# First batch's blocks enter the first layer five tiles later through a buffer of their own; unused work credit is kept and spent at up to three units a tile

## The chip, the cores and the metric

The kernel runs on one core of a Trainium2 chip. The metric is the device time of one execution in microseconds; lower is better. The engines named here are TensorE (PE, with its weight loads PEld), VectorE (DVE), ScalarE (ACT), GpSimd (POOL) and SyncE (SP), whose queue issues every DMA of this kernel.

## What is computed

Attention with queries averaged in pairs, then two feed-forward layers one after the other, all in float32 at the boundary:

```python
# q, k, v: (4, 8, 1152, 64); q_pool: (4, 8, 576, 64)
q_pool = q.reshape(B, H, S // 2, 2, D).mean(axis=3)
scores = np.matmul(q_pool, k.transpose(0, 1, 3, 2)) / np.sqrt(D)
attn = np.exp(scores - scores.max(-1, keepdims=True))
attn = attn / (attn.sum(-1, keepdims=True) + 1e-9)
x = np.matmul(attn, v)                    # -> (2304 tokens, 512)
h = x @ w_in;  g = h * np.cos(h);              x = g @ w_out    # layer 1, 512 -> 2048 -> 512
h = x @ w_in2; g = h * (1 / (1 + np.exp(-h))); x = g @ w_out2   # layer 2, 512 -> 2048 -> 512
```

## The kernel before

Every float32 operand of a matrix product is split into a high and a low float16 part, and three of the four partial products are taken.

**Attention.** A pair is one batch with heads j and j + 4; there are 16 pairs, four to a batch, numbered 0 to 15 here. A pair has nine tiles of 128 query rows, so the 144 tiles run in four batches of 36. For one tile: TensorE makes the scores (`sp`, L546; the fifth tile of a pair holds the rest of both heads and has twice the instructions, L554), VectorE scales them and takes the maximum (`sc`, L565), ScalarE takes the exponential (L573) and then the high part (`hl`, L579), GpSimd the low part (`hl`, L151), SP transposes both by DMA (`hlT<-hl`, L586), and TensorE multiplies by the values (`pv`, L597 and L601). `hl` is a ring of four buffers. The preparation of the next pair (`qn`, `kn`, `vt`, L467 and L472, and the transposes `qT`, `kT`) runs between the tiles as a background generator.

**Layer 1.** A finished batch gives two blocks of 256 tokens (blocks 0 and 1 from batch 0, up to 6 and 7 from batch 3), and the leftover rows of all batches give a ninth. A block has 16 H units (L682, twelve matmuls of 256 columns each) and 16 Y units (L742, also twelve). After two H units ScalarE takes two copies out of PSUM (`hk` L699, `tt` L703); after four of them come VectorE's steps (L716, L725, L730), a sine on ScalarE (L722) with a switch of its function table before it and one back to the exponential after it, and GpSimd's low part `gl`. The Y units of a block follow its H units by 12 units (`LG`). Before its first unit a block is split by `x_split`: maximum, scale, `xn` (ScalarE L664 and VectorE L665) and a DMA transpose `xT<-xn` (L668). In the kernel before, `xn` is taken from the `hl` ring.

**Who sets the order.** The tile loop (at L1070 and after) writes the program: scores, exponential, high and low part, then `advance()`, which steps every background generator once, and `share()`, which emits layer-1 units from a credit. `advance()` is called four times a tile. In batches 1 to 3 each half tile adds one credit (`RATE` is 2 a tile). A unit spends one; credit is capped at 4, and when no block is in `blocks_q` the units wait. A block of batches 1 to 3 waits another 40 steps (`X_LAG`, ten tiles) after `x_split` before it is put in `blocks_q`; blocks 0 and 1 do not wait. A scheduler then reorders each engine's queue by priorities, so the built order differs from the written one, but each engine runs its own queue in order.

**After attention** come the remaining units of layer 1, in a loop that takes one unit and one step of the preparation of layer 2's weights (`wgen2`), and then layer 2 (`ys`, `gs`, `op`).

Of the kernel before, what the change touches and what calls it, by code (L numbers as in the profile page):

```python
# [12 lines left out]
F16 = mybir.dt.float16  # L13
# [12 lines left out]
PSH = 15.0  # L26
NB_SC, NB_H, NB_T, NB_S = 4, 4, 4, 5
LOW_HL, LOW_G, LOW_W = 3, 2, 2
X_LAG = 40
W1_BUFS, WT_BUFS = 3, 3  # L30
W1_TABLE = (6, (0, 2, 4, 8, 11), 2)
W2_BUFS, W2_PACE = 3, 6
# [16 lines left out]
def attention_moe_moe_kernel(ctx, tc, q, k, v, w_in1, w_out1, w_in2, w_out2, out):  # L49
# [6 lines left out]
    DM, DFF = w_in1.shape  # L56
# [569 lines left out]
    def moe_pools(stack):  # L626
        mp = Weights()
        mp.p = stack.enter_context(tc.tile_pool(name="moe", bufs=2, reuse_waits="tile"))
        return mp
# [24 lines left out]
    def x_split(at, mp, x32, i, blk, w):  # L654

        m = small.tile([128, 1], F32, name="xm", tag="xm")
        absmax(m, x32, AX.XY)
        yield
        s = small.tile([128, 1], F32, name="xs", tag="xs")
        u = small.tile([128, 1], F32, name="xu", tag="xu")  # L660
        yield from early(scale_steps(m, ps_h, (s, u), 14), P_CH)
        blk.c = x_scale_consts(w, s, u, True)
        xn = at.p.tile([128, 2, 2, DM], F16, tag="hl", name="xn", bufs=NB_H)
        nc.scalar.activation(out=xn[:, 0], in_=x32, func=AF.Copy, scale=s)  # L664
        nc.vector.scalar_tensor_tensor(out=xn[:, 1], in0=x32, scalar=s, in1=xn[:, 0], op0=ALU.mult, op1=ALU.subtract)  # L665
        yield
        blk.T = mp.p.tile([128, 2, 2, NC, 128], F16, tag="x%d" % i, name="xT", bufs=1)
        nc.sync.dma_start_transpose(  # L668
            out=blk.T.rearrange("p e t c k -> p (e t c) k"), in_=xn.rearrange("p e t d -> p (e t d)")
        )  # L670
        blk.xh = lambda c: blk.T[:, 0, :, c, :]
        blk.xl = lambda c: blk.T[:, 1, :, c, :]
# [210 lines left out]
    if True:  # L883
# [6 lines left out]
        at = att_pools(att_stack)  # L890
# [3 lines left out]
        make_consts()  # L894

        state = Weights()
        state.mp = None
        state.ng, state.tail = 0, False
        state.psw = ps_h
        W2 = new_w("2", 8, True)  # L900
        state.credit = 0.0
        bg = []
        blocks_q = []

# [5 lines left out]
        def finish(g):  # L910
            while g in bg:
                advance()
# [35 lines left out]
        units = layer1()  # L948

        def share(x):  # L950
            if state.mp is None:
                return
            state.credit = min(state.credit + x, 4.0)
            while state.credit >= 1 and next(units, False):
                state.credit -= 1

        pairs = [(b, j) for b in range(B) for j in range(NP)]
# [27 lines left out]
        xgens = {}  # L985

        def block_steps(b, i):
            blk = Block()
            blk.g = []
            blk.ydst = ydr[2 * b + i]  # L990
            yield from early(x_split(at, state.mp, x32.pop((b, i)), i, blk, W1), P_X)
            if b:
                for _ in range(X_LAG):
                    yield
            blocks_q.append(blk)

        def x_of(b, i):
# [6 lines left out]
        def block_done(b, i):  # L1004
            if state.mp is None:
                finish(wg)
                wst_stack.close()
                state.mp = moe_pools(moe_stack)
            xgens[b, i] = block_steps(b, i)
            bg.append(xgens[b, i])  # L1010

# [40 lines left out]
        for n, (b, j) in enumerate(pairs):  # L1052


            seq = list(range(2 * NT))
            if j == NP - 1:
                seq = [t + NT * e for t in range(NT) for e in range(2)]
            seq.insert(NT, 2 * NT)
            order = []
            for o in range(0, len(seq), GT):  # L1060
                G = Pair()
                G.P, G.tiles = P.get(n), seq[o:o + GT]
                order += [(G, i, t) for i, t in enumerate(G.tiles)]
            if n + 1 < len(pairs):
                bg.append(prep_then_load(n + 1))
            else:
                at.src_stack.close()
                w2st_stack = ExitStack()
                w2st = w2st_stack.enter_context(tc.tile_pool(name="w2st", bufs=1, reuse_waits="tile"))
                wgen2 = layer2_weight_steps(W2, (w_in2, w_out2), w2st, lambda: state.psw, nc.sync, W2_BUFS, W2_TABLE)  # L1070
                bg.append(slowly(islice(wgen2, 4), W2_PACE))
            for idx, (G, gi, t) in enumerate(order):
                with ahead(P_SC):
                    T = tile_scores(at, P[n], t)
                T.G, T.gi = G, gi
                inflight.append(T)
                with ahead(P_EX):
                    tile_exp(at, T)
                tile_hi(at, T, b == 0 or (idx % HI_N) < HI_A)
                tile_lo(at, T)  # L1080
                advance()
                share(RATE[b] / 2)
                advance()
                if len(inflight) > LAG:
                    drain_pv()
                advance()
                share(RATE[b] / 2)
                advance()
# [184 lines left out]
```

## Time and profile before

| | us |
|---|---|
| median of the 3 runs shown | 1331.56 (1325.54 to 1332.42) |
| the profiled execution, whole | 1323.71 |
| its span, first to last instruction | 1321.9 |
| attention, batch 0 (tiles 0 to 35) | 0 to 231.4 |
| batch 1 (tiles 36 to 71) | 231.4 to 427.0 |
| batch 2 (tiles 72 to 107) | 427.0 to 603.1 |
| batch 3 (tiles 108 to 143) | 603.1 to 784.6 |
| rest of layer 1, then layer 2 | 784.6 to 1321.9 |

A stage begins here with the first exponential (L573) of its first tile and ends with that of the next stage; the last boundary is the exponential of the last tile. The busy time of TensorE counts each matmul from its start to its modelled end, and matmuls overlap; what one costs in a full queue is the distance from its start to the next one's.

### The profile page before, as it was taken

To read this page: it belongs to the slowest core of one execution; us is meant where nothing else is said; L and a number is where in the kernel's file an instruction comes from. 1 tells how busy PE (TensorE), PEld (TensorE's weight loads), DVE (VectorE), ACT (ScalarE), POOL (GpSimd) and SP (SyncE) were. 2 spreads that over 40 slices of the span, in tenths; PEclk is the share of its full clock that TensorE was granted. 3 is DMA by queue.
4 is the path that set the end of the run, shared out by engine and by line. 5 is a ranking of instruction groups with operands and counts; after the bars stand their busy time and mean duration, and the time that the engine had idled before them with its cause. 6 is when DMAs were issued, how large, how long until landed. Compare 5 with 4: busy or idle time off the path is not lost. (4 is left out here: it accounts for less than half of the span.)

```text
span 1321.9 us, 26728 instructions
## 1 busy us (share of the span) xinstructions
PE 1130.4 (86%) x10668; PEld 912.1 (69%) x10668; DVE 953.3 (72%) x1876; ACT 938.5 (71%) x1147; POOL 708.6 (54%) x624
## 2 busy tenths in 40 slices
PE   2565566889897789899989999899988999999998
PEld 1343343577685567676767679788877888888887
DVE  7787888777776877896779866976677754544483
ACT  4887988789887889997999884664556534443351
POOL 1768677668877667786868882444777100000000
PEclk9766665899999889998999899999999999999999
DMA  9899999868899999998999974413534000000001
GB/s 294 174 221 219 235 250 192 141 146 163 149 214 193 193 185 190 201 172 181 203 199 188 202 136 104 129 55 65 108 94 97 17 33 33 9 9 17 17 34 32
DMA packets 491165, 181.57 MB, mean 137 GB/s; under 512 B 447520, under 2 KB 465952, under 8 KB 491040
## 3 DMA queue, kind: packets, MB, share of 16 engines
q1 hardware_dynamic: 491040, 179.87, 65.5%
q8 instruction: 83, 1.36, 0.4%
q14 instruction: 42, 0.34, 0.1%
HBM read 66.58 MB, written 9.44 MB: 58 GB/s over the span
## 5 line engine op out<-in xcount | busy, mean ns | idle before, releaser
L151 POOL TENSOR_TENSOR hl<-sc,hl 128x384 f16<-128x384 f32 x432 | 450.7, 1074 | 125.6 <-ACT hl L579 92.6
L546 PE MATMUL sp<-kT,qT 128*128 128x512 f16 (+1 forms) x768 | 197.8, 378 | 85.5 <-DVE sc L565 73.9
L565 DVE TENSOR_SCALAR_CACHE_REDUCE sc<-sp,psu 128x512 f32<-128x512 f32 (+1 forms) x288 | 228.2, 808 | 58.3 <-PE sp L546 45.9
L682 PEld LDWEIGHTS <-ih 128*128 128x128 f16 x2304 | 225.5, 99 | 48.4 <-issue 18.1
L597 PE MATMUL pv<-vt,hlT 128*128 128x130 f16 (+1 forms) x1440 | 192.3, 237 | 49.8 <-DMA hlT<-hl 43.2
L573 ACT ACTIVATE sc<-sc,nb 128x1152 f32<-128x1152 f32 x144 | 179.2, 1250 | 46.4 <-DVE nb L570 33.1
L682 PE MATMUL h<-ys,ih 128*128 128x256 f16 x1152 | 194.0, 273 | 8.5 <-ACT gs L699 8.5
L597 PEld LDWEIGHTS <-hlT 128*128 128x128 f16 (+1 forms) x1440 | 146.7, 110 | 78.5 <-DMA hlT<-hl 50.6
L682 PE MATMUL h<-xT,ih 128*128 128x256 f16 x1024 | 188.0, 278 | 7.0 <-ACT tt L703 5.1
L601 PE MATMUL pv<-vt,hlT 128*128 128x65 f16 (+1 forms) x1440 | 182.7, 207 | 0.0
L546 PEld LDWEIGHTS <-qT 128*128 128x128 f16 x768 | 77.5, 110 | 152.0 <-issue 100.0
L579 ACT ACTIVATE hl<-sc 128x1152 f16<-128x1152 f32 x144 | 164.4, 1154 | 8.8 <-DMA hlT<-hl 4.6
L742 PE MATMUL y<-gh,oh 128*128 128x256 f16 x576 | 158.6, 275 | 4.8 <-ACT y L751 4.8
L742 PE MATMUL y<-gl,oh 128*128 128x256 f16 x576 | 158.5, 275 | 2.1 <-POOL gl L151 2.1
L856 PEld LDWEIGHTS <-op 128*128 128x128 f16 x1512 | 147.9, 98 | 17.9 <-issue 0.6
L742 PE MATMUL y<-gh,ol 128*128 128x256 f16 x576 | 158.6, 275 | 0.0
L682 PE MATMUL h<-ys,il 128*128 128x256 f16 x576 | 157.0, 273 | 0.0
L601 PEld LDWEIGHTS <-hlT 128*128 128x128 f16 (+1 forms) x1440 | 142.5, 108 | 16.1 <-issue 8.1
L682 PE MATMUL h<-xT,il 128*128 128x256 f16 x512 | 142.5, 278 | 0.0
L151 POOL TENSOR_TENSOR gl<-tt,gh 128x512 f16<-128x512 f32 (+1 forms) x60 | 102.8, 1728 | 60.8 <-DVE gh L730 58.6
L742 PEld LDWEIGHTS <-oh 128*128 128x128 f16 x1152 | 112.6, 99 | 24.2 <-issue 7.0
L682 PEld LDWEIGHTS <-il 128*128 128x128 f16 x1152 | 113.6, 99 | 15.2 <-issue 0.3
(311 smaller groups left out, 2007.7 us busy)
## 6 DMA issues: line engine op xcount, KB each, us to landing
wst<-in_moe_w_in_dram SPq DMA_DIRECT2D x16, 1024.0 KB, 6.4
stk<-in_k_dram SPq DMA_DIRECT2D x32, 288.0 KB, 4.2
stv<-in_v_dram SPq DMA_DIRECT2D x32, 288.0 KB, 4.3
stq<-in_q_dram SPq DMA_DIRECT2D x32, 256.0 KB, 3.2
wst<-in_moe_w_out_dram SPq DMA_DIRECT2D x8, 1024.0 KB, 6.2
wst<-in_moe_w_out_dram SPq DMA_DIRECT2D x16, 512.0 KB, 6.3
ydr<-y SPq DMA_DIRECT2D x9, 512.0 KB, 3.6
y32b<-ydr SPq DMA_DIRECT2D x9, 512.0 KB, 3.3
```

The source lines that it names most:

```text
L151: last = nc.gpsimd.tensor_tensor(out=lo[:, o:o + w], in0=x[:, o:o + w], in1=hi[:, o:o + w], op=ALU.subtract)
L546: nc.tensor.matmul(sp[:, o - a:o - a + n], P.qT[e][:, t, :], kT[:, o:o + n], start=(e == 0), stop=(e == 1))
L565: nc.vector.tensor_scalar(out=T.sc[:, a:z], in0=sp, scalar1=T.P.su, scalar2=None, op0=ALU.mult, op1=ALU.min, accum_out=mx[:, x:x + 1],)
L573: nc.scalar.activation(out=T.sc, in_=T.sc, func=AF.Exp, scale=-1.0, bias=nb)
L579: nc.scalar.activation(out=hi, in_=T.sc, func=AF.Copy)
L597: nc.tensor.matmul(G.pv[r, T.gi], T.hlT[:, 0, c, r], P.vt[i][:, c], start=(c == 0), stop=(c == KC - 1), skip_group_check=True,)
L601: nc.tensor.matmul(G.pv[r, T.gi, 0], T.hlT[:, 1, c, r], P.vt[i][:, c, 0], start=False, stop=(c == KC - 1), skip_group_check=True,)
L682: nc.tensor.matmul(hp, wt[:, c, f * 128:(f + 1) * 128], xt(c), start=(i == 0), stop=(i == 3 * NC - 1), skip_group_check=True,)
L742: nc.tensor.matmul(blk.y[:, oc, :], wt[:, f, oc * 128:(oc + 1) * 128], gt[:, f % 4, :], start=(f == 0 and e == 0 and oc % 2 == 0), stop=(f ...
L856: nc.tensor.matmul(bank, t[:, e, c, :], wt[:, c, :], start=start, stop=True, skip_group_check=True)
```

## The change

The wait before a block enters layer 1 becomes `(20, 40)`: 20 steps, five tiles, for batch 0's blocks, 40 as before for the others. `xn` comes from a pool of its own with one buffer from the first finished block until the last pair of heads begins, so the blocks of batches 0 to 2 no longer take a buffer of the `hl` ring; those of batch 3 still do. The credit is capped at 14 instead of 4, and a half tile spends at most 1 or 2 of it in turn, so a tile at most 3.

```diff
-X_LAG = 40
+X_LAG = (20, 40)
...
-        xn = at.p.tile([128, 2, 2, DM], F16, tag="hl", name="xn", bufs=NB_H)
+        if state.xp is None:
+            xn = at.p.tile([128, 2, 2, DM], F16, tag="hl", name="xn", bufs=NB_H)
+        else:
+            xn = state.xp.tile([128, 2, 2, DM], F16, name="xn", bufs=1)
...
-            state.credit = min(state.credit + x, 4.0)
-            while state.credit >= 1 and next(units, False):
+            state.credit = min(state.credit + x, 14.0)
+            state.turn = 3 - state.turn
+            for _ in range(state.turn):
+                if state.credit < 1 or not next(units, False):
+                    return
                 state.credit -= 1
...
-            if b:
-                for _ in range(X_LAG):
-                    yield
+            for _ in range(X_LAG[b > 0]):
+                yield
...
+                state.xp = xn_stack.enter_context(tc.tile_pool(name="xn", bufs=1, reuse_waits="tile"))
...
             else:
                 at.src_stack.close()
+                for i in range(2):
+                    finish(xgens[b - 1, i])
+                xn_stack.close()
+                state.xp = None
```

Three places in the built order. The first is ScalarE's queue at the start of batch 1, from the exponential of tile 39 on. `xn` is the split of a block, `qn`, `kn`, `vt` and `qT` are the preparation of pair 5, `hk` and `tt` are the copies that follow H units. Before:

```order
L573 ACTIVATE sc<-sc,nb 128x1152
L664 ACTIVATE xn<-x_532,xs 128x1024
L579 ACTIVATE hl<-sc 128x1152
L620 ACTIVATE x_533<-pvs,den 128x64 x3
L573 ACTIVATE sc<-sc,nb 128x1152
L579 ACTIVATE hl<-sc 128x1152
L573 ACTIVATE sc<-sc,nb 128x1152
L579 ACTIVATE hl<-sc 128x1152
L573 ACTIVATE sc<-sc,nb 128x1152
L699 ACTIVATE hk<-h,ca 128x512
L703 ACTIVATE tt<-h,quarter,ca 128x512
```

After:

```order
L573 ACTIVATE sc<-sc,nb 128x1152
L467 ACTIVATE qn<-stq,ps__2447 128x9x64
L467 ACTIVATE kn<-stk,ps__2447 128x9x64 x2
L467 ACTIVATE vt<-stv,ps__2447 128x9x64
L579 ACTIVATE hl<-sc 128x1152
L467 ACTIVATE vt<-stv,ps__2447 128x9x64
L620 ACTIVATE x_533<-pvs,den 128x64 x3
L573 ACTIVATE sc<-sc,nb 128x1152
L579 ACTIVATE hl<-sc 128x1152
L667 ACTIVATE xn<-x_532,xs 128x1024
```

The preparation of pair 5, which stood behind the first two sines before, now stands ahead of the first block's `xn`, and the first `hk` has moved back by nine rows of this queue.

The second place is ScalarE's queue around the second block's `xn`, a few tiles later in batch 1. Before, it is followed by three rows `hl` that share its ring:

```order
L573 ACTIVATE sc<-sc,nb 128x1152
L722 ACT_TABLE_LOAD
L722 ACTIVATE tt<-tt,halfpi 128x1024
L664 ACTIVATE xn<-x_533,xs 128x1024
L579 ACTIVATE hl<-sc 128x1152 x3
L699 ACTIVATE hk<-h,ca 128x512
L703 ACTIVATE tt<-h,quarter,ca 128x512
```

After:

```order
L573 ACTIVATE sc<-sc,nb 128x1152 x2
L620 ACTIVATE x_2669<-pvs,den 128x64 x2
L667 ACTIVATE xn<-x_533,xs 128x1024
L579 ACTIVATE hl<-sc 128x1152 x2
L573 ACTIVATE sc<-sc,nb 128x1152
L702 ACTIVATE hk<-h,ca 128x512
L706 ACTIVATE tt<-h,quarter,ca 128x512
```

Both blocks are now split before the first H unit is copied out, and the sine stands behind them.

The third place is TensorE's queue just after the last attention tile, where `bm` is a small product that spreads a column's maximum over the partitions (`xm` of block 7, `mrem` of the leftover rows, `mw` of a weight piece). Before, Y units stand between these and the first H unit:

```order
L742 MATMUL y<-gh,ol_86 128x256
L110 MATMUL bm<-xm,mean 128x1
L110 MATMUL bm<-mrem,mean 128x1
L742 LDWEIGHTS oh_85
L742 MATMUL y<-gh,oh_85 128x256
L742 LDWEIGHTS oh_85
L742 MATMUL y<-gl,oh_85 128x256
```

After:

```order
L745 MATMUL y<-gh,ol_86 128x256
L110 MATMUL bm<-ym,mean 128x1
L110 MATMUL bm<-mw,mean 128x1
L110 MATMUL bm<-xm,mean 128x1
L110 MATMUL bm<-mrem,mean 128x1
L110 MATMUL bm<-mw,mean 128x1
L685 LDWEIGHTS ih_83
L685 MATMUL h<-xT,ih_83 128x256
```

The five small products now stand together, with 13 matmuls of Y units between them and the last `pv` (84 before the first H unit in the kernel before), and block 6's 16 H units follow them in one run.

## Rows read from the trace of the kernel before

**Rows 1.** The page's head: the span, and the engines' busy time

```profile
span 1321.9 us, 26728 instructions
PE 1130.4 (86%) x10668; PEld 912.1 (69%) x10668; DVE 953.3 (72%) x1876; ACT 938.5 (71%) x1147; POOL 708.6 (54%) x624
```

**Rows 2.** Busy time by stretch (batches 1, 2, 3, rest); last columns: clock, DMA, GB/s

```profile
231.40:427.00 195.60, 169.12 (x1697) 129.37 (x1694) 145.74 (x326) 166.75 (x199) 146.56 (x132) 0.97 0.86 167
427.00:603.10 176.10, 152.72 (x1595) 116.86 (x1596) 141.11 (x315) 163.69 (x199) 128.51 (x124) 0.93 1.01 192
603.10:784.60 181.50, 168.56 (x1688) 128.39 (x1686) 148.62 (x316) 161.58 (x193) 140.43 (x125) 0.95 0.93 182
784.60:1321.90 537.30, 515.45 (x4752) 458.57 (x4749) 329.49 (x486) 263.48 (x361) 140.38 (x95) 1.00 0.22 55
```

**Rows 3.** The same view for pairs 4, 7 and 11 (columns PE, PEld, DVE, ACT, POOL)

```profile
231.40:294.40 63.00, 52.80 (x506) 40.52 (x504) 45.42 (x103) 50.40 (x61) 38.64 (x35) 0.92 0.74 141
392.30:427.00 34.70, 25.97 (x279) 19.01 (x277) 25.18 (x66) 27.48 (x34) 26.98 (x27) 0.96 0.95 185
562.00:603.10 41.10, 38.50 (x424) 30.45 (x424) 34.47 (x75) 40.63 (x51) 33.84 (x32) 1.00 1.03 190
```

**Rows 4.** Timeline of ScalarE in pair 4: start, duration, in brackets idle time before

```profile
251.69 1.25 ACT L573 ACTIVATE sc<-sc,nb 128x1152 f32<-128x1152 f32 x1 [0.54 <-DVE nb L570]
257.57 0.69 ACT L699 ACTIVATE hk<-h,ca 128x512 f32<-128x512 f32 x1 [4.62 <-PE h L682]
...
260.19 0.69 ACT L699 ACTIVATE hk<-h,ca 128x512 f32<-128x512 f32 x1 [1.26 <-PE h L682]
...
280.59 3.26 ACT L579 ACTIVATE hl<-sc 128x1152 f16<-128x1152 f32 x3
...
290.29 1.16 ACT L579 ACTIVATE hl<-sc 128x1152 f16<-128x1152 f32 x1 [3.73 <-DMA xT<-xn]
```

**Rows 5.** Timeline of GpSimd in pair 4

```profile
266.90 2.89 POOL L151 TENSOR_TENSOR gl<-tt,gh 128x512 f16<-128x512 f32 x2 [12.97 <-DVE gh L730]
278.28 1.40 POOL L477 TENSOR_TENSOR stq<-stq 128x576 f32<-128x576 f32 x1 [8.49 <-DMA stq<-in_q_dram]
281.88 11.35 POOL L151 TENSOR_TENSOR hl<-sc,hl 128x384 f16<-128x384 f32 x9 [2.20 <-ACT hl L579]
```

**Rows 6.** Timeline of TensorE: a tile's scores, then values; a Y unit's start and its successor's

```profile
259.99 1.14 PE L546 MATMUL sp<-kT,qT 128*128 128x512 f16 x6
260.96 0.22 PE L597 MATMUL pv<-vt,hlT 128*128 128x130 f16 x1
...
261.94 0.38 PE L682 MATMUL h<-xT,ih 128*128 128x256 f16 x2
...
784.39 0.27 PE L742 MATMUL y<-gh,oh 128*128 128x256 f16 x1
...
785.70 0.38 PE L682 MATMUL h<-xT,ih 128*128 128x256 f16 x2
```

**Rows 7.** ScalarE's groups in batches 1 to 3: count, busy us and mean ns

```profile
L703 ACT ACTIVATE tt<-h,quarter,ca 128x512 int32<-128x512 f32 x47 | 35.8, 768 | 1.7 <-DMA ydr<-y 1.5 <-POOL gl L151 0.2
L699 ACT ACTIVATE hk<-h,ca 128x512 f32<-128x512 f32 x47 | 31.7, 675 | 11.4 <-PE h L682 11.3
L722 ACT ACT_TABLE_LOAD x22 | 28.2, 1283 | 0.4
L573 ACT ACT_TABLE_LOAD x22 | 28.2, 1283 | 6.5 <-DVE den L613 3.0 <-DVE pm L489 1.8 <-DVE nb L570 1.3
...
L722 ACT ACTIVATE tt<-tt,halfpi 128x1024 f32<-128x1024 f32 x23 | 26.4, 1148 | 1.7 <-DVE tt L716 1.5
```

**Rows 8.** After the last tile: last `pv`, block 7's maximum, TensorE's first longer wait

```profile
799.84 0.19 PE L601 MATMUL pv<-vt,hlT 128*128 128x65 f16 x1
...
804.61 1.22 DVE L128 TENSOR_REDUCE xm<-x 128x1 f32<-128x1024 f32 x1 [0.31 <-ACT x L620]
...
831.45 0.38 PE L682 MATMUL h<-xT,ih 128*128 128x256 f16 x2 [2.14 <-ACT tt L703]
```

More of the change, by code (lines that the diff above doesn't have):

```diff
@@ L896, in attention_moe_moe_kernel @@
         state = Weights()
-        state.mp = None
+        state.mp = state.xp = None
+        xn_stack = ExitStack()
         state.ng, state.tail = 0, False
@@ L901, in attention_moe_moe_kernel @@
         state.credit = 0.0
+        state.turn = 1
         bg = []
```

## The prediction, made before the changed kernel ran

> **What bounds the kernel now.** I read the page's head first [rows 1], then busy time by stretch, since no engine is the bound over the whole span. After the last tile TensorE is busy 515 of 537 us (last of [rows 2]): there time follows its matmuls. In batches 1 to 3 nothing is full over a batch: ScalarE has 166.8 of 195.6, 163.7 of 176.1 and 161.6 of 181.5 us [rows 2]. Pair by pair it looks different. Pair 11, with 15 units, has ScalarE busy 40.63 of 41.10 us; pair 7, with no H unit, has it busy 27.48 of 34.70 [rows 3]. So a pair with many H units is bound by ScalarE, and one with none has a floor of about 34.7 us that no single engine fills. Then I looked at batch 1, which is longest though its units are no more than in batch 2. Its first pair takes 63.0 us with ScalarE busy only 50.4 [rows 3]. The timelines show why: after the exponential at 251.69 ScalarE waits 4.62 us for TensorE to finish a run of H units and 1.26 us for the next, and later 3.73 us because `hl` wants a buffer that the block's `xn` still holds, until its transpose has landed [rows 4]. GpSimd has no attention tile from about 254 to 282: it waits 12.97, 8.49 and 2.20 us [rows 5]. Call this the hole.
>
> **Prices.** A unit costs TensorE 1.31 us (784.39 to 785.70), a tile 0.97 for the scores and 0.98 for the values [rows 6]; nine tiles with the odd tile's second set make 19.5 us a pair. An H unit costs ScalarE (0.768 + 0.675) / 2 = 0.72 for the copies, 1.148 / 4 = 0.29 for the sine, and 44 table loads of 1.283 over 92 units (23 sines) = 0.61, together 1.62 us [rows 7]. With pair 7's 27.5 as the base, 8 H units give 27.5 + 13.0 = 40.5, against 40.63 in pair 11 [rows 3], so the price fits. A pair's floor is then the largest of 19.5 + 1.31 x units, 27.5 + 1.62 x H units, and 34.7.
>
> **Part 1: the start of batch 1 (lag of five tiles, own buffer).** In the new order the preparation of pair 5 comes ahead of the blocks' split, both blocks are split before the first `hk`, and no `hl` row has to wait for `xn`. The wait of 3.73 us goes. The two waits behind a run of H units (4.62 and 1.26) should go too: before, the units were overdue in the written order when the transposed block arrived, and TensorE's queue has four and then eight of them in a row; now runs of four remain, but the next tiles stand ready ahead of them. That is 9.6 us of ScalarE's idle time, the engine that sets the pace here. Bounds: nothing, if the hole only moves to pair 5; and 24.8 us, which is all that batch 1 takes above the floors of its four pairs (46.9 + 45.3 + 42.1 + 36.5 = 170.8, from units counted in TensorE's order, against 195.6). The whole hole as GpSimd sees it is 23.7 us [rows 5], close to that end; but ScalarE did the units' and the preparation's work in it, which has to be done anyway, so I take the 9.6. The new buffer is single: the second `xn` waits for the first one's transpose. Between them ScalarE has about nine rows, some 9 us by its durations in [rows 4] and [rows 7], so I cost this wait at nothing; if that cover were gone it would be up to the 3.7 us that was saved, once in a batch, with exponentials queued behind it. SP's queue keeps its transposes; `xT` moves behind `qT` and `kT`, which are wanted first. The lag itself delays nothing that anyone waits for: batch 1's units still end at about tile 62 of the written order, seventeen tiles before the next block is due.
>
> **Part 2: kept credit, up to three units a tile.** This takes no work away; it packs it. In TensorE's new order the pairs of batch 1 have 4, 29, 18 and 13 units (15, 19, 17, 13 before), those of batch 2 have 4, 17, 20, 14 (3, 13, 17, 13), those of batch 3 have 14, 16, 20, 15 (18, 14, 16, 15). With the prices above the floors go from 170.8 to 172.2, 164.4 to 166.5 and 168.7 to 169.2: +4.0 us. The dense pairs are then bound by TensorE as much as by ScalarE (45.8 and 43.8 us for pair 10), where ScalarE alone was; the pairs with few units sit on the 34.7 us floor and give nothing back. What batches 2 and 3 take above their floors now (11.7 and 12.8 us) I leave as it is. Bounds: 0 (the floors' model adds too much), and +8 us for each of batches 2 and 3, half of the 16.1 us that pair 4 takes above its floor of 46.9, if their new dense pairs run as unevenly as pair 4 did. The nearest row is pair 11, which runs evenly with two units a tile, so I take +4.0.
>
> ScalarE's order has two more table loads (49 against 47): 2 x 1.283 = 2.6 us [rows 7], which is in the 0.61 per unit. The Trainium skill (ScalarE: Activation LUTs, What ACT_TABLE_LOAD costs) adds a drain of about 1.38 us to each switch, 2.66 us in all; by that the two would cost 5.3 us. The traced groups show 0.4 us of idle time before 22 loads [rows 7], so the drain isn't seen there and I go by the row.
>
> **Part 3: what is left after attention.** After the last tile's first score matmul TensorE has 404 H and 768 Y matmuls of layer 1's paired blocks in the old order, 384 and 668 in the new: 120 fewer at 1.31 / 12 = 0.109 us, 13.1 us, where TensorE sets the time. Not all of it is kept, as these units covered something. Block 7's chain from the last `pv` (799.84) to the end of its maximum (804.61 + 1.22) takes 5.8 us [rows 8]; 84 Y matmuls (9.2 us) covered it, now 13 (1.4 us). TensorE stands at the five `bm` for 1.7 us (a chain of bare durations, about 3.1) to 4.4 us: I take 3.0. All H units queue behind. Then block 6's 16 H units run in one piece, 21.0 us, while ScalarE's rows for them, with layer 2's weight pieces in between, sum to some 26 us; with two PSUM tiles of slack I take 3.6 us of waiting, less the 2.1 us that stood at this place before [rows 8], +1.5. Together -13.1 + 3.0 + 1.5 = -8.6. Bounds: -13.1 and 0.
>
> **Sum.** -9.6 + 4.0 - 8.6 = -14.2 us. The profiled execution took 1323.7 us, span 1321.9 [rows 1]; it would come to 1309.5. The median shown, 1331.56, lies 7.9 us above that execution. I take the difference from the median: 1317.4 us. With its own bounds the forecast spans 1308 to 1325.
>
> **Rivals.** (a) *The hole moves to pair 5.* For it: pair 5's order has 19 H units, more than pair 4 ever had, and runs of four still stand ahead of scores. Against: its tiles have their preparation done. Then part 1 gives 0: 4.0 - 8.6 = -4.6, 1327.0 us. Much the same comes if part 3 gives nothing because layer 2's weights are ready last: -9.6 + 4.0 = -5.6, 1326.0. Both are within 0.5% of the median (1324.9 to 1338.2), about what a measurement of this kernel can tell from no change. (b) *Slower: packing costs more than it moves.* One mechanism: at three units a tile TensorE runs units while VectorE waits for scores, and each dense start of batches 1 to 3 pays a hole. Batch 1 then keeps its own; batches 2 and 3 pay 8.05 each (half of 16.1): 16.1 + 4.0 - 8.6 = +11.5, 1343 us. It decides from 5.6 us each, which takes the sum past +6.6 us. For it: pair 4 shows that price [rows 3]. Against: the first ten tiles of batches 2 and 3 have nearly the same H units in both orders.
> The Trainium skill (Perfetto Trace Analysis, Optimization Strategy) says that stages with different bounds may gain from being interleaved; packing parts them, into tiles with three units and tiles with none. By that rule the time would come out as in (b); the trace agrees in direction, as pairs 7 and 11 show, but the +4.0 of part 2 is all that its rows give.
> (c) *More is gained*: batch 1 loses all its excess and part 3 is kept whole: -24.8 + 4.0 - 13.1 = -33.9, 1298 us. For it: GpSimd's hole is that long [rows 5]. (d) *The kept credit finds no work*: in the written order the blocks are used up at tile 140 with 8 credits left, so at most a few units more could leave the end. This is in part 3's count already and no case of its own.
>
> **How the numbers follow.** Forecast 0.50, (c) 0.10, (a) 0.26, (b) 0.14. Faster by over 0.5%: 0.60; within: 0.26; slower: 0.14. The range runs from 1302, inside (c), to 1338, which takes in (a) and leaves out most of (b).
>
> **What would show it.** Right: in pair 4 no wait of `hl` for `xT<-xn`, no idle time over 3 us of ScalarE or over 6 us of GpSimd between tiles 39 and 46, batch 1 at 183 to 191 us; batches 2 and 3 within 4 us of 176 and 181; the rest after the last exponential 7 to 11 us shorter, with a wait of 2 to 4 us at the five `bm`. Wrong: pair 5 above 66 us (the hole moved), pairs 10 or 14 above 50 (packing), or the rest unchanged in length with longer waits of `h` for ScalarE.

## The result, and the profile of the changed kernel

The changed kernel takes 1340.93 us (median of 4 runs, 1335.01 to 1343.96), the kernel before 1328.55 in runs beside it: a ratio of 1.0106, 95% interval 1.007 to 1.0143. It is about 1% slower, outside the range of 1302 to 1338, and close to the 1343 us of rival (b). The profiled execution took 1335.01 us.

The page's head, against [rows 1]: TensorE's and ScalarE's work is nearly the same, the span is 11.3 us longer.

```profile
span 1333.2 us, 26712 instructions
PE 1130.7 (85%) x10668; PEld 909.0 (68%) x10668; DVE 960.8 (72%) x1876; ACT 943.3 (71%) x1149; POOL 693.0 (52%) x624
```

Busy time by stretch (batches 1, 2, 3, rest; after the length come PE, PEld, DVE, ACT, POOL, then clock, DMA share, GB/s), against [rows 2]:

```profile
232.60:428.50 195.90, 171.38 (x1715) 130.54 (x1714) 147.39 (x327) 168.04 (x200) 135.47 (x132) 0.93 0.86 169
428.50:614.50 186.00, 168.00 (x1668) 125.19 (x1666) 144.00 (x316) 168.52 (x203) 137.10 (x128) 0.95 0.95 180
614.50:803.10 188.60, 170.72 (x1747) 131.94 (x1747) 150.05 (x320) 164.02 (x197) 133.54 (x126) 0.96 0.94 182
803.10:1333.20 530.10, 501.27 (x4596) 446.15 (x4593) 323.71 (x479) 258.86 (x353) 131.74 (x90) 0.99 0.21 53
```

These windows begin 0.6 us after the exponentials that mark the stages (231.95 for batch 1, 802.5 for the last tile). That leaves the batches' lengths as they are, but the rest is 530.7 us from its mark. So batch 1 is what it was (195.6 to 195.9 us), batch 2 is 9.9 us longer, batch 3 is 7.1 longer, and the rest is 6.6 shorter. A stage of one profile is good to a few us only: batch 0, where the kernels with whole transposes run the same work, took between 201.3 and 207.6 us in their profiles. Two kernels below whose engines run the same rows in the same order in all their stages (lag and lag20) differ by 0.7 to 2.1 us in batches 1 to 3 and by 4.3 in batch 0.

The same view for pairs 4, 5, 10 and 14 of the changed kernel:

```profile
232.60:274.50 41.90, 30.65 (x260) 20.42 (x259) 35.19 (x87) 36.01 (x44) 31.21 (x32) 0.76 0.93 164
274.50:339.10 64.60, 60.08 (x618) 49.25 (x616) 48.31 (x92) 56.18 (x66) 40.52 (x39) 1.00 0.81 163
517.50:571.30 53.80, 51.27 (x489) 38.46 (x486) 37.95 (x82) 46.06 (x54) 39.89 (x38) 0.97 0.86 159
708.30:763.70 55.40, 51.66 (x502) 38.80 (x499) 42.92 (x84) 49.20 (x58) 43.09 (x40) 1.00 0.91 183
```

and for pairs 5, 10 and 14 of the kernel before:

```profile
294.40:339.80 45.40, 38.33 (x382) 29.75 (x382) 35.05 (x76) 42.51 (x51) 39.09 (x36) 1.00 0.91 179
520.10:562.00 41.90, 38.11 (x403) 30.03 (x400) 36.65 (x77) 40.59 (x50) 32.33 (x33) 0.96 1.03 201
700.80:742.20 41.40, 39.85 (x434) 31.94 (x433) 35.86 (x72) 40.75 (x47) 35.62 (x34) 1.00 1.08 215
```

Pair 4 fell from 63.0 us [rows 3] to 41.9, but pair 5 rose from 45.4 to 64.6, with TensorE busy 60.08 of it. Pairs 10 and 14 rose from 41.9 and 41.4 us to 53.8 and 55.4; TensorE is busy 95% and 93% of them, ScalarE no longer all the time. The granted clock isn't the cause: it is 0.97 and 1.00 there, 0.96 and 1.00 before. The other pairs of batches 2 and 3 changed by -4.1 to +2.0 us, by 9 us downward together. So in this profile the loss of batches 2 and 3 sits in two pairs, each the third of its batch.

What the engines wait for in pair 10 of the changed kernel (the waits: total us, times, longest):

```profile
POOL hl L151 <- ACT hl L579: 6.7, 1, 6.7
DVE sc L565 <- PE sp L546: 6.4, 1, 6.4
POOL gl L151 <- DVE gh L733: 5.0, 2, 3.8
ACT hk L702 <- PE h L685: 3.4, 1, 3.4
```

and in pair 10 of the kernel before, the waits of the same two readers of scores and of `hl`:

```profile
DVE sc L565 <- PE sp L546: 2.2, 2, 1.6
POOL hl L151 <- ACT hl L579: 1.6, 2, 1.2
```

VectorE stands 6.4 us once for a tile's scores, until 528.30, while TensorE works off units and value products, and ScalarE then stands 3.4 us for H units (until 530.06). GpSimd's wait of 6.7 us comes 22 us later (until 551.07), behind ScalarE's part of the next pair's preparation, and doesn't follow from this one. In pair 14 the wait for scores is 4.1 us at one place, where the longest before was 0.8. That is the mechanism of rival (b), but in the third pair of a batch, not at its dense start. The first four tiles of pair 10, one line each:

```profile
517.50:524.80 7.30, 7.30 (x55) 4.67 (x52) 3.76 (x8) 7.24 (x8) 7.30 (x7) 1.00 0.87 163
524.80:532.00 7.20, 7.20 (x63) 5.27 (x63) 2.33 (x6) 3.72 (x5) 4.81 (x6) 1.00 0.45 84
532.00:538.20 6.20, 6.20 (x65) 4.36 (x64) 5.49 (x13) 6.11 (x6) 4.84 (x4) 1.00 0.52 95
538.20:545.00 6.80, 6.80 (x76) 5.60 (x74) 6.03 (x12) 6.80 (x12) 4.72 (x5) 1.00 0.74 117
```

TensorE is busy all 27.5 us of them, with 11 of the pair's 20.9 units in these tiles; in the five tiles after them it is busy 23.8 of 26.3 us. Before, the whole pair had 15.4 units.

### The profile page after: what moved, and what is told of

Read it like the earlier page. It is cut to its first block, busy times and chain, and to the rows that moved or that the text cites. A ratio compares the mean times of both kernels' runs of the same rounds, so it can differ in the third digit from the quotient of the medians.

```text
span 1333.2 us, 26712 instructions
## 1 busy us (share of the span) xinstructions
PE 1130.7 (85%) x10668; PEld 909.0 (68%) x10668; DVE 960.8 (72%) x1876; ACT 943.3 (71%) x1149; POOL 693.0 (52%) x624
## 5 line engine op out<-in xcount | busy, mean ns | idle before, releaser
L151 POOL TENSOR_TENSOR hl<-sc,hl 128x384 f16<-128x384 f32 x432 | 443.7, 1058 | 132.4 <-ACT hl L579 97.0
L685 PE MATMUL h<-xT,ih 128*128 128x256 f16 x1024 | 192.4, 281 | 8.3 <-ACT tt L706 5.9
L597 PEld LDWEIGHTS <-hlT 128*128 128x128 f16 (+1 forms) x1440 | 144.2, 109 | 69.9 <-DMA hlT<-hl 42.8
L601 PE MATMUL pv<-vt,hlT 128*128 128x65 f16 (+1 forms) x1440 | 185.5, 205 | 0.0
L601 PEld LDWEIGHTS <-hlT 128*128 128x128 f16 (+1 forms) x1440 | 140.3, 107 | 15.7 <-issue 6.6
L151 POOL TENSOR_TENSOR gl<-tt,gh 128x512 f16<-128x512 f32 (+1 forms) x60 | 92.5, 1558 | 72.8 <-DVE gh L733 72.8
```

The source lines that it names most:

```text
L151: last = nc.gpsimd.tensor_tensor(out=lo[:, o:o + w], in0=x[:, o:o + w], in1=hi[:, o:o + w], op=ALU.subtract)
L597: nc.tensor.matmul(G.pv[r, T.gi], T.hlT[:, 0, c, r], P.vt[i][:, c], start=(c == 0), stop=(c == KC - 1), skip_group_check=True,)
L601: nc.tensor.matmul(G.pv[r, T.gi, 0], T.hlT[:, 1, c, r], P.vt[i][:, c, 0], start=False, stop=(c == KC - 1), skip_group_check=True,)
L685: nc.tensor.matmul(hp, wt[:, c, f * 128:(f + 1) * 128], xt(c), start=(i == 0), stop=(i == 3 * NC - 1), skip_group_check=True,)
```

## The experiments

Eighteen kernels ran; the six that leave work out stand further down. "Y units carried" is the number of Y matmuls between the first exponential of batch 1 and the last one, divided by 12; the length is that of batches 1 to 3, both from one profile of each. Of the paired blocks' 128 H and 128 Y units every kernel carries 95 or 96 H units there.

| kernel | what it is | ratio to before (95%) | Y carried | batches 1, 2, 3 (us) | sum |
|---|---|---|---|---|---|
| before | | 1 | 82.2 | 195.6, 176.1, 181.5 | 553.2 |
| after | whole change | 1.0106 (1.007 to 1.0143) | 89.1 | 195.9, 186.0, 188.6 | 570.5 |
| lag | lag alone | 0.9926 (0.9902 to 0.9949) | 82.3 | 194.2, 178.2, 174.7 | 547 |
| lag20 | lag of 5 tiles everywhere | 0.9939 (0.9917 to 0.9962) | 82.2 | 192.1, 178.9, 176.5 | 548 |
| buf | buffer alone | 0.9958 (0.9936 to 0.998) | 83.2 | 197.1, 176.3, 178.8 | 552 |
| lag_buf | lag and buffer | 0.997 (0.995 to 0.9991) | 83.0 | 192.6, 176.8, 177.0 | 546 |
| credit | credit part alone | 1.0086 (1.0057 to 1.0116) | 90.0 | 198.5, 187.4, 188.6 | 575 |
| keep | cap of 14 alone | 1.01 (1.0069 to 1.0131) | 90.2 | 198.6, 190.4, 187.9 | 577 |
| turn | limit of 3 a tile alone | 1.0051 (1.0028 to 1.0074) | 82.0 | 196.1, 180.4, 177.3 | 554 |
| pack2 | credit part in batch 2 alone | 1.0096 (1.0074 to 1.0118) | 83.1 | 196.4, 186.0, 177.3 | 560 |
| rate225 | 2.25 credits in batch 3 | 1.0038 (1.0021 to 1.0054) | 86.5 | 199.1, 175.1, 187.8 | 562 |
| even | one unit a half tile | 1.0138 (1.0117 to 1.0158) | 80.0 | 199.6, 186.2, 181.8 | 568 |
| spread | lag, 1.75 credits in batches 1, 2 | 0.9978 (0.9959 to 0.9996) | 82.2 | 187.5, 177.8, 184.3 | 550 |
| spread1 | lag, 1.75 credits in batch 1 | 0.9964 (0.9943 to 0.9985) | 83.2 | 189.6, 173.7, 183.1 | 546 |

### The parts of the change

**lag**: in the kernel before, nothing else than

```diff
-X_LAG = 40
+X_LAG = (20, 40)
...
-            if b:
-                for _ in range(X_LAG):
-                    yield
+            for _ in range(X_LAG[b > 0]):
+                yield
```

> The lag alone: xn from the hl ring, old credit. Theory H with the buffer as its cause: batch 1 within 4 us of before, as hl still waits for xn. Theory H with the lag as its cause: batch 1 shorter by 6 to 12 us. Theory P: within 5 us of before as a whole.

**buf**: the buffer of its own, no lag (`X_LAG = (0, 40)`), old credit.

> The own buffer alone: no lag for the first batch, old credit. Theory H with the buffer as its cause: the wait of hl for xT<-xn (3.7 us) is gone and batch 1 is shorter by 3 to 10 us. Theory P: within 5 us of before as a whole. Theory L: slower, as the second xn waits for the first one's transpose on ScalarE.

**lag_buf**: the changed kernel with the old credit,

```diff
-            state.credit = min(state.credit + x, 14.0)
-            state.turn = 3 - state.turn
-            for _ in range(state.turn):
-                if state.credit < 1 or not next(units, False):
-                    return
+            state.credit = min(state.credit + x, 4.0)
+            while state.credit >= 1 and next(units, False):
```

> The lag of five tiles and the own buffer for xn, with the old credit (cap 4, no packing). Theory P (packing pays nothing back: the credit alone makes the slowdown): batches 2 and 3 return to about 176 and 181 us, batch 1 stays near 196 or a little below; the whole is 0 to 10 us faster than before. Theory H (the prediction's part 1, a gain of about 10 us hidden by the credit's cost): batch 1 is 183 to 191 us and the whole 8 to 14 us faster. Theory L (the lag or the buffer costs something too): slower than before by over 3 us.

**credit**: these lines the other way, in the kernel before.

> The kept credit with up to three units a tile alone: first batch's blocks enter at once, xn from the hl ring. Theory P: slower than before by 10 to 16 us, with batches 2 and 3 longer by about 10 and 7 us, the rest after attention about 7 us shorter, batch 1 as before (195.6 us). Theory H: slower by over 18 us. Theory L: slower by under 6 us.

Lag and buffer gain 0.3 to 0.7%; the credit alone gives most of the loss, 1.0086 of 1.0106. The lag alone is faster than both kernels, 1317.7 us: more than the 5 us that its theory P allowed, and not by theory H, since batch 1 is 1.4 us shorter instead of 6 to 12. In its profile the gain sits in batch 3 (181.5 to 174.7 us); no run here shows why. buf took 0.4% off the whole and nothing off batch 1, where 3 to 10 us were expected. Its batches 2 and 3 and those of credit:

```profile
425.60:603.80 178.20, 155.51 (x1648) 120.10 (x1645) 143.71 (x321) 163.83 (x200) 132.25 (x125) 0.97 1.03 192
603.80:778.50 174.70, 160.01 (x1673) 123.79 (x1673) 143.86 (x313) 160.33 (x191) 138.99 (x123) 1.00 0.98 185
```

```profile
432.20:619.60 187.40, 168.22 (x1683) 125.85 (x1682) 142.95 (x316) 169.52 (x204) 131.78 (x126) 0.95 0.92 179
619.60:808.20 188.60, 169.12 (x1710) 130.43 (x1711) 146.62 (x319) 163.57 (x194) 132.72 (x126) 0.96 0.92 178
```

The lag carries some 25.6 Y units in batch 2 (308 matmuls, 19 units before), one more than credit (24.6), without its loss: 6.5 of them fall into pair 8, where no block of the batch is ready yet. So it isn't the number in a batch.

**lag20**: `X_LAG = (20, 20)`, the blocks of all batches five tiles late.

> The lag alone (no buffer, old credit), with five tiles for the blocks of every batch instead of five and ten: the units of batches 2 and 3 start five tiles earlier, at two a tile, so more units leave the end without packing. Theory P: the whole is faster than with the lag alone (1317.7) by 0 to 10 us. Theory M: no gain over the lag alone, or a loss, as moved units cost as much in attention as they save at the end.

In the traces its order is that of lag row for row on TensorE, ScalarE, VectorE and GpSimd. It ran like lag, and says nothing on the later batches' lag; what it gives is a second profile of the same order.

### Which half of the credit part

**pack2**: credit, but in batch 2 only (against credit; the lines that keep the batch's number in `state.b` are left out):

```diff
-            state.credit = min(state.credit + x, 14.0)
+            pack = state.b == 2
+            state.credit = min(state.credit + x, 14.0 if pack else 4.0)
...
-            for _ in range(state.turn):
+            n = state.turn if pack else 4
+            for _ in range(n):
```

> The kernel before with the kept credit and up to three units a tile in batch 2 alone; batches 1 and 3 spend as before. Theory P (packing itself costs): batch 2 is longer by 8 to 12 us, batch 3 about as before or a few us shorter, the whole slower by 4 to 12 us. Theory M (what costs is the units moved from the end into attention): nearly nothing is moved from the end, so the whole is within 3 us of before.

**keep**: the kernel before with

```diff
-            state.credit = min(state.credit + x, 4.0)
+            state.credit = min(state.credit + x, 14.0)
```

> Half of part 2 alone: credit is kept up to 14 units, with no limit on what a half tile spends. In TensorE's order batch 2 has 25.6 Y units in place of 16, pairs 9 and 10 have 19 and 15 units, and 14 units fewer are left after attention (32 H and 57 Y against 35 and 64). Theory T (units brought into pairs that TensorE or ScalarE fills cost their full price): as slow as credit, 1338 to 1343 us, with batch 2 at 184 to 188. Rival (the limit of three a tile, which cuts units into alternating pieces, makes the loss): 1320 to 1330.

**turn**: the cap stays at 4;

```diff
-            while state.credit >= 1 and next(units, False):
+            state.turn = 3 - state.turn
+            for _ in range(state.turn):
+                if state.credit < 1 or not next(units, False):
+                    return
                 state.credit -= 1
```

> The other half alone: credit capped at 4 as before, and one or two units spent in a half tile in turn. Batch 1 and the rest after attention are those of the kernel before; in batches 2 and 3 hardly a unit more is emitted before the end, and pair 10 has 20 units in TensorE's order (17 before). Theory T: near the kernel before, 1326 to 1333, with pair 10 some 3 us longer. Rival (the limit makes the loss): 1338 or more.

**rate225**: `RATE = (0, 2, 2, 2.25)`.

> The kernel before with 2.25 credits a tile in batch 3 instead of 2, cap 4: the end keeps as many units as in the changed kernel in the written order, with the added units spread evenly over batch 3. Theory M: batch 3 is longer by 7 us or more, the rest shorter by 4 to 7, the whole slower than before or the same. Theory P: batch 3 longer by under 4 us, the whole the same or up to 4 us faster.

Keeping the credit makes the loss: keep is as slow as the whole change, with batch 2 at 190.4 us (184 to 188 expected). The limit alone costs half a per cent. pack2 points to a loss without more units in all: it carries 83.1 Y units, but 5.6 of batch 3's in batch 2, which takes 9.9 us longer, while batch 3 gives 4.2 back. The other 9 us by which its profile is longer than that of the kernel before lie outside batches 2 and 3: 4.3 in batch 0, whose order is the same, 0.8 in batch 1, and 4.0 after attention, where some two units fewer were left. rate225 carries 4.3 units more, in the full batch 3, for 6.3 us there, and gives 1.4 back after attention, where 4 to 7 were expected. The Y units of batch 2 in the kernel before, the changed kernel and keep (the window of that line alone; PE and its count):

```profile
427.00:603.10 176.10, 31.42 (x228) 21.81 (x228) 0.93 1.01 192
```

```profile
428.50:614.50 186.00, 41.15 (x299) 28.83 (x299) 0.95 0.95 180
```

```profile
429.70:620.10 190.40, 44.21 (x320) 31.66 (x320) 0.95 0.94 182
```

**even**: credit left from a wait isn't spent in one burst:

```diff
-            while state.credit >= 1 and next(units, False):
+            if state.credit >= 1 and next(units, False):
```

> The kernel before with at most one unit a half tile (no burst of four when blocks arrive): less packing, and three H units more at the end. Theory P: batches 2 and 3 the same or shorter by up to 6 us, the rest longer by 2 to 4 us, the whole within 4 us of before. Theory M: attention shorter by as much as the rest is longer or more, the whole up to 4 us faster. Too close to tell the two apart alone; it shows whether the packing price goes on below two units a tile.

**spread** and **spread1**: lag with `RATE = (0, 1.75, 1.75, 2)` and `(0, 1.75, 2, 2)`.

> The opposite of packing: the lag alone (blocks 0 and 1 five tiles later, old credit), and 1.75 credits a tile in batches 1 and 2 in place of 2, so that units of a batch run on into the first pair of the next one, where no block is ready yet. In TensorE's order pair 10 has 11 units (20 with the lag alone), pair 8 has 15 (11), pair 12 has 17 (15), and the rest after attention is unchanged (35 H and 64 Y). Theory T (units cost their price in pairs that are full and little in those that are not): batch 2 at 172 to 177, the whole at 1308 to 1316, faster than the lag alone (1317.7). Rival (density makes no difference by itself, the lag gained only by closing the hole): within 0.2% of the lag alone, 1315 to 1321.

> The lag alone with 1.75 credits a tile in batch 1 only. Pair 8 has 15 units in TensorE's order (11 with the lag alone), pair 10 has 18 (20), the rest after attention is unchanged. Theory T: 1312 to 1318, between the lag alone and the version with 1.75 in both batches. Rival: within 0.2% of the lag alone, 1315 to 1321.

Here the theory that only full pairs cost fell short. even is the least packed and the slowest kernel, outside both of its forecasts. The two spread kernels do shorten batches 1 and 2 (to 365 and 363 us together, lag 372), but the units that they put off come back in batch 3, 8 to 10 us longer than with the lag, and as medians both are slower than the lag. Thinning units out is no gain by itself.

### What sets the pace: three cuts

**before_23, after_23**: the third partial product of each layer-1 unit left out (8 matmuls of 12), here of the Y units:

```diff
-            for e, (wt, gt) in enumerate(((w.oh, gh), (w.oh, gl), (w.ol, gh))):
+            for e, (wt, gt) in enumerate(((w.oh, gh), (w.oh, gl))):
```

> The kernel before, with the third partial product of every layer-1 unit left out (8 of 12 matmuls a unit stay). Theory T (a packed stretch is bound by TensorE): this takes TensorE's bound away from packed pairs, so the kernel after with the same cut is within 4 us of this one. Theory A (it is ScalarE, or latency, that packing costs): the difference between the two stays 9 to 15 us. On its own: 60 to 130 us shorter than before, most of it after attention.

> The changed kernel with the same cut. Theory T: within 4 us of the cut kernel before. Theory A: 9 to 15 us longer than that.

1313.87 and 1313.12 us: 0.9913 (0.9884 to 0.9941) and 0.991 (0.9877 to 0.9943). The gap between the kernels is gone, as a TensorE bound would have it, but the gain of 12 to 14 us is far under the 60 to 130 expected. The test is also weaker than it looked. These are the Y units of batches 1 to 3 with the cut, before and after (eight matmuls to a unit):

```profile
236.10:428.90 192.80, 32.39 (x256) 24.29 (x256) 0.91 0.90 172
428.90:617.60 188.70, 34.53 (x252) 25.69 (x252) 0.88 0.94 182
617.60:799.90 182.30, 33.12 (x247) 24.66 (x248) 0.88 0.93 181
```

```profile
233.80:420.00 186.20, 35.29 (x256) 25.19 (x256) 0.88 0.91 169
420.00:610.80 190.80, 35.05 (x256) 24.86 (x256) 0.90 0.98 191
610.80:791.30 180.50, 35.80 (x256) 25.31 (x256) 0.92 0.93 180
```

Both carry nearly all of their 96 units (755 and 768 matmuls), so the change had hardly anything left to bring forward. Part of the expected gain was spent in attention: by the same rows the cut kernel's three batches take 563.8 us, 10.6 more than the kernel before, with 12 Y units more in them and a granted clock of 0.88 to 0.91 instead of 0.93 to 0.97.

**before_ns, after_ns**: a plain copy in the place of the sine, which takes the function-table switches away:

```diff
-            nc.scalar.activation(out=G.t, in_=G.t, func=AF.Sin, scale=-2.0 * math.pi, bias=halfpi)
+            nc.scalar.activation(out=G.t, in_=G.t, func=AF.Copy, scale=-2.0 * math.pi)
```

> The kernel before with a plain copy in the place of the sine, so that ScalarE switches no table in attention (about 44 loads of 1.28 us fewer). Theory A with ScalarE as the cause: the changed kernel with the same edit is within 4 us of this one. Theory T: it stays 9 to 15 us longer. On its own: 10 to 40 us shorter than before.

> The changed kernel with a plain copy in the place of the sine. Theory A with ScalarE as the cause: within 4 us of the kernel before with the same edit. Theory T: 9 to 15 us longer than that.

1324.3 us, 0.9979 (0.9958 to 0.9999), and 1341.12, 1.011 (1.0072 to 1.0147). The gap stays. Batch 2 of the kernel before without the switches:

```profile
428.30:607.30 179.00, 154.48 (x1576) 116.79 (x1576) 139.89 (x317) 145.16 (x186) 129.31 (x122) 0.94 1.01 191
```

ScalarE is busy 145.2 us in place of 163.7, and the batch isn't shorter; the whole was expected to gain 10 to 40 us. ScalarE's work doesn't bound this batch, whatever its busy share says. The Trainium skill (ScalarE: Activation LUTs, What ACT_TABLE_LOAD costs) puts 2.66 us on a switch, its drain included; the load itself takes 1.283 us [rows 7], and 45 fewer loads in the whole kernel (47 to 2) moved it by 3 us.

**before_lo, after_lo**: only the low part of the exponentials is transposed, both products read it:

```diff
-            out=T.hlT.rearrange("p e c k -> p (e c) k"), in_=T.hl.rearrange("p e s -> p (e s)")
+            out=T.hlT[:, 1], in_=T.hl[:, 1, :]
...
-                    G.pv[r, T.gi], T.hlT[:, 0, c, r], P.vt[i][:, c],
+                    G.pv[r, T.gi], T.hlT[:, 1, c, r], P.vt[i][:, c],
```

> Kernel before with half of the attention's transposes left out: only the low part of the exponentials is transposed, and both products with the values read it (their count and the order of the work stay; the output is not the reference's). New theory D: the floor of about 35 us that a pair with few units has, and which no engine fills, is the DMA queue's own work. The DMA engines' busy share is 1.01 in batch 2 and 1.03 in batch 0, where there are no units at all, and length times share is 168 to 178 us in every batch. D expects batch 0 to fall from 203 us to 172 to 185 (ScalarE and VectorE are busy 170 to 172 us there) and batches 2 and 3 to 165 to 175, the whole to 1270 to 1300. Rival: the floor is the chain from tile to tile (scores, maximum, exponential, parts, transpose, values), in which a transpose that takes 5 us becomes only somewhat shorter: batches within 5 us of before, the whole 1315 to 1330.

> The same cut in the changed kernel (low part alone is transposed, both products with the values read it). D: packing loses because the pairs with few units can't use the time they are given (they stand at the DMA floor) while the dense pairs stand on TensorE; without the floor the sparse pairs give the time back, and the gap of 13 us to the kernel before falls below 5. Rival (dense stretches lose by themselves, by alternation and waits on TensorE in pairs 5, 10 and 14): pair 5 stays above 60 us, pairs 10 and 14 above 50, and the gap stays 10 us or more.

1300.77 us, 0.9794 (0.9765 to 0.9824), and 1316.44, 0.9911 (0.9882 to 0.9941). Batches 0 and 2, and pair 7, of the first:

```profile
29.50:225.50 196.00, 114.97 (x948) 73.36 (x948) 171.97 (x402) 170.86 (x187) 150.16 (x135) 0.70 0.79 176
413.20:586.30 173.10, 151.11 (x1602) 114.94 (x1599) 139.68 (x321) 162.72 (x198) 127.84 (x123) 0.97 0.69 137
378.10:413.20 35.10, 33.34 (x364) 25.67 (x363) 26.25 (x67) 28.58 (x35) 28.88 (x30) 0.92 0.77 144
```

The whole is 26 us faster, between the two forecasts, and neither fits all batches: batch 0 is 196.0 us (203.3 before), not D's 172 to 185, and batches 1 to 3 are 7.9, 3.0 and 5.3 us shorter, where the rival said within 5. The reading that length times DMA share is 168 to 178 us in every batch holds for batches 1 to 3; in batch 0 it is 209 (203.3 x 1.03). The DMA share of batch 2 falls from 1.01 to 0.69, yet the batch loses 3 us, and pair 7 none (34.7 before, [rows 3]) with its share at 0.77. So the DMA engines are not the floor of that sparse pair, but shorter transposes do shorten batches somewhat. The gap between the kernels, 15.7 us, stays, as the rival said; of its marks pairs 5 (63.9 us) and 14 (51.0) hold, and pair 10, at 46.4 us in place of over 50, does not.

### What follows

The loss comes with kept credit: with it credit, keep and pack2 are about 1% slower, and without it the changed kernel (lag_buf) isn't slower at all. Leaving out ScalarE's switches or half of the transposes leaves the gap between the kernels as it is. That the credit costs by what it brings forward is argued, not shown. From the table, and as an estimate from one profile of each, a Y unit brought into attention before its end makes batches 1 to 3 longer by (570.5 - 553.2) / (89.1 - 82.2) = 2.5 us in the changed kernel, 3.0 in keep and 2.1 in rate225, where it costs TensorE 1.31 [rows 6]; the rest of the changed kernel gives 6.6 us back for 6.9 Y units and one H unit. But even, which carries 2.2 Y units fewer, has batches 1 to 3 14 us longer, so the number of units doesn't set their length.

**What stays open** is why the price is twice TensorE's. Most of it can be read in pair 10: 5.5 units more than before are 7.2 us of the 11.9, and some 4 are the dear alternation of two shapes of matmul told of at the end (38 changes, 1 before). This is a rival that no run tests. In batch 2 such changes rose from 21 to 83 in the changed kernel, and to 81 in credit and pack2, 42 in keep and 58 in even; at the 0.11 us measured there, 62 more would be 6.8 us of the batch's 9.9. Against it: spread has 63 of them in batch 2, which takes 1.7 us longer than before, and in batch 3 of the changed kernel they fell from 103 to 74 while the batch took 7.1 us longer. Why even is slow isn't settled either: its batch 2 carries no more units than before and takes 10 us longer, of which 37 more changes would be 4.

## Why the prediction was wrong, step by step

**Part 1, the hole (-9.6): one wait went as said, the hole stayed, and nothing was gained.** In pair 4 and after, no row of `hl` waits for `xT<-xn` any more, as said. ScalarE's timeline around the first units:

```profile
264.08 1.15 ACT L667 ACTIVATE xn<-x,xs 128x1024 f16<-128x1024 f32 x1
265.14 1.15 ACT L579 ACTIVATE hl<-sc 128x1152 f16<-128x1152 f32 x1
266.91 1.16 ACT L579 ACTIVATE hl<-sc 128x1152 f16<-128x1152 f32 x1 [0.63 <-DMA hlT<-hl]
...
273.91 1.26 ACT L573 ACTIVATE sc<-sc,nb 128x1152 f32<-128x1152 f32 x1
...
285.03 0.69 ACT L702 ACTIVATE hk<-h,ca 128x512 f32<-128x512 f32 x1 [3.43 <-PE h L685]
...
288.94 1.26 ACT L573 ACTIVATE sc<-sc,nb 128x1152 f32<-128x1152 f32 x1
```

and the exponential that followed the one at 251.69 [rows 4] in the kernel before:

```profile
266.00 1.26 ACT L573 ACTIVATE sc<-sc,nb 128x1152 f32<-128x1152 f32 x1
```

The waits of 4.62 and 1.26 us for H units [rows 4] became 3.43 and 0.87; the 3.43 is over the 3 us that were set as a mark, and GpSimd's longest wait there, 7.34 us (until 292.70), is over its mark of 6. The hole itself is still there: 14.3 us between two exponentials before (251.69 to 266.00), 15.0 now (273.91 to 288.94), one pair later. Pairs 4 and 5 together went from 108.4 to 106.5 us with nearly the same units in them (24 H, 12 Y before and 11.4 now). The step that failed is that ScalarE's idle time is time saved since ScalarE "sets the pace here": the plain copy for the sine took 18.3 us of work off it in batch 1 without shortening the batch (195.6 to 196.7 us), and in pair 5 it is TensorE that is busy 60.08 of 64.6 us. A reading on the way to it was wrong too: batch 1's units are more than batch 2's, 64 against 51 in the trace, so part of its length is work and no hole. The units, five tiles later, all met in pair 5, which took 64.6 us where its floor by the prediction's formula was 58.3, and pair 4 with four units took 41.9 us, not 34.7, with TensorE busy 30.65 us of it; its granted clock was 0.76, where it had been 0.92 with 20 units. Batch 1's excess over its floors went from 24.8 to 195.9 - 172.2 = 23.7 us. That is rival (a) for this part, "the hole moves to pair 5". With the old credit, and so fewer units there (19.9 H, 7 Y), the two pairs take 97.1 us (lag_buf), but batch 1 as a whole is only 3.0 us shorter than before.

**Part 2, packing (+4.0): mis-sized.** Batches 2 and 3 measured +9.9 and +7.1, together +17.0. The floors were predicted to rise by 2.1 and 0.5; what they take above them, which I left "as it is", rose from 11.7 and 12.8 to 19.5 and 19.4. The bound of +8 a batch, drawn from pair 4, was near the right value (+7.8 and +6.6 above the floors), and the even run of pair 11 at two units a tile the wrong neighbour. One reason shows in pair 10: a floor over a whole pair takes the largest of three sums and so lets tiles without units make up for tiles with three, while TensorE was full in the first four tiles alone. The marks "pairs 10 or 14 above 50" were met. The Trainium skill (Perfetto Trace Analysis, Optimization Strategy) was on that side, with its gain from interleaving stages; but spread and even show that the trace agrees only as far as packing loses, and not that interleaving more gains.

**Part 3, the rest (-8.6): right in size, measured -6.6**, though its parts shifted. TensorE's timeline after the last tile, against [rows 8]:

```profile
817.45 0.38 PE L110 MATMUL bm<-xm,mean 128*128 128x1 f32 x2 [0.80 <-DVE ys L117]
...
834.17 0.59 PE L685 MATMUL h<-xT,ih 128*128 128x256 f16 x2 [5.39 <-ACT tt L706]
...
842.12 0.38 PE L685 MATMUL h<-xT,ih 128*128 128x256 f16 x2 [0.53 <-ACT tt L706]
```

TensorE waits about 1 us at the five `bm`, not 3.0; block 6's sixteen H units in one piece cost 5.39 + 0.53 = 5.9 us of waiting, not 3.6, since ScalarE's rows for layer 2's weights stand between their copies.

**The sum.** By rival (b), with +16.1 for batches 2 and 3, +4.0 and -8.6, came +11.5 us; measured, on the profiled executions, +11.3. That it is so close is partly luck: the sum was right, but the three batches cost 17.3 us more in place of 20.1, the rest gave 6.6 back in place of 8.6, and the loss sat in other pairs than the rival said. Its chance of 0.14 was too low. I weighed it down because the first ten tiles of batches 2 and 3 are alike in both orders; the loss came behind them, from the nineteenth tile on.

## What to carry to other kernels

Work that "only moves" has a price where it lands: bringing a unit forward pays only if the stretch that receives it has room on the engine that runs it, and a pair in which two engines are already busy over 90% has little. A floor is better taken over a few tiles than over a pair, since a stretch that is full isn't paid back by one that has room. An engine's idle time is worth saving only when taking that engine's work away is known to shorten the stretch, so test the pacing engine by cutting its work before pricing waits on it. When a change has separable parts, price them apart: here the lag alone was 0.7% faster and the credit alone 0.9% slower.

## What the runs showed of the hardware

I had not expected that alternating two kinds of matmul can cost so much. In the fifth tile of a pair the values use weights of 128 rows by 64 columns. Where they alternate with units of 128 by 128 (changed kernel, pair 10; TensorE's timeline):

```profile
521.63 0.28 PE L685 MATMUL h<-xT,ih 128*128 128x256 f16 x1
521.85 0.24 PE L597 MATMUL pv<-vt,hlT 128*64 128x130 f16 x1
522.02 0.28 PE L685 MATMUL h<-xT,il 128*128 128x256 f16 x1
522.24 0.22 PE L601 MATMUL pv<-vt,hlT 128*64 128x65 f16 x1
522.39 0.28 PE L685 MATMUL h<-xT,ih 128*128 128x256 f16 x1
```

and where both have 128 columns (pair 5):

```profile
289.76 0.27 PE L745 MATMUL y<-gl,oh 128*128 128x256 f16 x1
289.87 0.19 PE L601 MATMUL pv<-vt,hlT 128*128 128x65 f16 x1
289.90 0.27 PE L745 MATMUL y<-gh,ol 128*128 128x256 f16 x1
290.01 0.22 PE L597 MATMUL pv<-vt,hlT 128*128 128x130 f16 x1
```

Around the value product of 65 columns it is 0.37 us from a unit's start to the next one's above (522.02 to 522.39) and 0.14 below (289.76 to 289.90): each of the two changes of shape costs some 0.11 us. The Trainium skill (TensorEngine Tiling (Array Packing), Key Properties) says that changing the tiling mode drains TensorE; the trace agrees in that each change costs time, with this number beside it. The kernel before has 154 such changes between units and value products, at this price 17 us of TensorE's time, the changed kernel 182, 20 us; in pairs 10 and 14 they rose from 9 to 88, and 26 of them stand in the 6.4 us for which VectorE waits in pair 10. No run here took them out, so what they are worth in time is not known.
